# A fused attention and expert kernel: other PSUM banks and another engine for weights at the passage to the experts

## The chip, the cores and the metric

The kernel runs on one core of a Trainium2 chip as a single program. The metric is the device time of that program in microseconds (us). The core has five engines, each with a queue of its own that it works off in order: TensorE (PE, matmuls and transposes), VectorE (DVE), ScalarE (ACT), GpSimd (POOL) and SyncE (SP, which here only issues transfers). Matmul results go to PSUM, which is used here as eight banks of 512 columns; tiles of one tag in a pool share a fixed number of banks, so a new tile waits until the engine that reads the old one is done.

## The reference, cut to what matters

```
# 1. attention, B=4, 8 heads, S=576, head size 64; four heads see the last 32 positions,
#    four see the positions of their own residue modulo 32
x = softmax(mask(q @ k.T / 8)) @ v                     # -> (4, 576, 512)
# 2. mixing layer
theta = x @ w_theta;  zr = x * cos(theta);  zi = x * sin(theta)
y = w_tok_r @ zr + w_tok_i @ zi;  u = x + y
x = u + relu(u @ w_ch)                                 # (4, 576, 512)
# 3. four experts, each a causal attention with its own projections; two are chosen per position
logits = x @ w_gate;  chosen = the two largest;  w = softmax of the two
out = sum over chosen e of  w_e * (softmax(causal(q_e @ k_e.T / 8)) @ v_e @ wo_e)
```

## The kernel before

Most matmuls are carried out as three products of split operands: each operand is a high part, rounded to fp32r, and a low part, the rest. `mm3` issues high by high, high by low and low by high into one bank. Each high part is a copy on ACT or DVE, each low part a subtraction on DVE or POOL.

The program has two phases. In the first, the four batches b = 0 to 3 go through `theta` (angles), `rotate` (`xn` transposes, z), `tokens` (y, 27 matmuls into one bank of the tag "acc", which has two banks; each unit is evicted on DVE at L375 into X) and `channels` (g, evicted at L397). The attention of batch b+1 is interleaved in four pairs of heads (`attn_pair`): scores, exp on ACT (L227), transposes `tp` (L239), their copy `pt` on ACT (L243). The sine of `theta` and the exp lie in different tables of ACT, so that going from one to the other loads a table. In the second phase each batch goes through V products (`pv`, `project_v`), q and k products of two experts at a time (`pq_b_m_part_n`: m the pair of experts, part 0 q and part 1 k, n the half of the positions), and for each expert `attention` with scores s, masks, exp, transposes tp, values o; fills put products of later work between the score matmuls.

Between the phases lies the passage: while the last batch's `tokens` run, `load_split` brings in the weights wqk (four blocks of 512 columns) and wvg (four of 260: V and gate) through three stage buffers. SP issues a block's transfer when a buffer is free, ACT writes the high part (L106), and an engine writes the low part (L108), which frees the buffer. Then come the last `channels` units, the five V units of batch 0 (the fifth, `pv_4`, holds the ends of batches 0 and 1, and ACT copies the second as `v_end`), the choice of experts `gates(0)` on DVE, the q and k units of experts 0 and 1, and the weights wo. A q unit is evicted in four steps: ACT copies the first head's high part (L578), DVE writes its low part from the same bank (L579), and so again for the second head. A k unit goes the same way (L582, L583).

The order of the instructions on each engine is set by a planner that simulates the program; program text sets it only in part. `tc.issue_after(x)` adds the rule that the instructions in its block come after x in the queue of x's engine; it adds no wait between engines. Pools are opened and closed as stacks, and pool `ps2` of the second phase takes the banks that `ps1` of the first phase leaves, in the order in which its tags are first used: before, "acc" (two banks), "s" (three), "t" (two, for transposes), "o" (one), so that the V and q products take the banks in which the first phase's "acc" lay.

## Time and profile before

| | |
|---|---|
| runs | 548.86, 549.3 and 2792.86 us, median 549.3 |
| profiled execution | 548.84 us, span 547.1 us |
| mean granted TensorE clock | 0.982 |
| PE busy | 523.8 us (96% of the span) |
| DVE busy | 399.3 us (73%) |
| ACT busy | 316.8 us (58%) |
| POOL busy | 195.2 us (36%) |

The span runs from the first to the last instruction; 1.7 us of the execution lie outside it. Of the three runs two lie within 0.5 us of each other, and one is far off. A share of busy time is an average over all stages; of TensorE, 523.8 us of 547.1 us leave 23.3 us in which it did no work, and the views below show where some of these lie.

### The profile page before, as it was taken

How to read it: one execution, taken by the hardware profiler on the slowest of the kernel's cores; microseconds unless marked ns; L12 is line 12 of the kernel's file. 1: busy time of each engine (PE TensorE's matmuls, PEld its weight loads, DVE VectorE, ACT ScalarE, POOL GpSimd, SP SyncE). 2: the span in 40 equal slices, each digit the busy share in tenths (PEclk: the TensorE clock that was granted, in tenths of full speed). 3: DMA queues.
4: the chain of work that ended last, by engine and by line, in shares of the span. 5: the costliest groups of instructions: out<-in, count | busy, mean ns of one | idle time of the engine just before them, and what ended most of it. 6: DMA issues, size and time to landing. Idle time of an engine off the chain costs nothing.

```text
span 547.1 us, 12352 instructions
## 1 busy us (share of the span) xinstructions
PE 523.8 (96%) x4500; PEld 499.2 (91%) x4500; DVE 399.3 (73%) x1237; ACT 316.8 (58%) x874; POOL 195.2 (36%) x280
## 2 busy tenths in 40 slices
PE   6899889999999999999999999999999999999997
PEld 5788889999999999989999999879988998999987
DVE  6979997585847567756456443699998888888972
ACT  4878965336363263452145431587788757867873
POOL 5100023230643113542006453175456443625541
PEclk9859999999999999999999999999999999999999
DMA  9857255360202131000100021000001001100112
GB/s 269 280 186 261 61 183 160 112 205 1 87 6 88 34 134 34 23 23 15 46 0 2 3 58 40 1 1 2 1 22 54 14 2 44 45 2 10 36 46 88
DMA packets 20133, 36.62 MB, mean 67 GB/s; under 512 B 2648, under 2 KB 12040, under 8 KB 20072
## 3 DMA queue, kind: packets, MB, share of 16 engines
q1 hardware_dynamic: 20072, 35.83, 20.3%
q8 instruction: 36, 0.59, 0.5%
q14 instruction: 25, 0.20, 0.1%
HBM read 31.10 MB, written 4.72 MB: 65 GB/s over the span
## 4 chain that ended last, share of the span: by engine, by line
PE 72%; DVE 15%; ACT 6%; DMA 4%; issue 3%; POOL 0%; SPq 0%; DVEq 0%; ACTq 0%; POOLq 0%
PE y L290 6%; PE y L291 6%; PE y L292 6%; PE av L267 4%; PE g L290 3%; PE g L292 3%; PE g L291 3%; PE s L203 3%; PE tp L672 3%; PE tp L239 3%; PE th L290 3%; PE th L292 3%; PE th L291 2%; PE pq L290 2%; PE s L631 2%
## 5 line engine op out<-in xcount | busy, mean ns | idle before, releaser
L290 PE MATMUL y<-wtk_hi,zhi 128*128 128x288 f32 x288 | 86.0, 300 | 1.8 <-DVE X L375 1.2
L291 PE MATMUL y<-wtk_lo,zhi 128*128 128x288 f32 x288 | 85.5, 298 | 0.0
L292 PE MATMUL y<-wtk_hi,zlo 128*128 128x288 f32 x288 | 85.5, 298 | 0.0
L236 POOL TENSOR_TENSOR p<-p,sm 128x288 f32<-128x288 f32 (+2 forms) x36 | 22.6, 634 | 135.8 <-DVE sm L235 58.7
L667 POOL TENSOR_SCALAR p<-p,sm,gt 128x256 f32<-128x256 f32 (+3 forms) x63 | 44.9, 715 | 53.7 <-DVE sm L665 25.1
L290 PEld LDWEIGHTS y<-wtk_hi,zhi 128*128 128x128 f32 x288 | 54.0, 188 | 2.5 <-DVE X L375 1.6
L291 PEld LDWEIGHTS y<-wtk_lo,zhi 128*128 128x128 f32 x288 | 54.1, 188 | 0.1
L292 PEld LDWEIGHTS y<-wtk_hi,zlo 128*128 128x128 f32 x288 | 54.0, 188 | 0.0
L360 POOL TENSOR_TENSOR zlo<-cs,zhi 128x512 fp32r<-128x512 f32 (+1 forms) x30 | 36.0, 1213 | 49.0 <-DVE zhi L356 41.3
L290 PE MATMUL th<-wth_hi,x_hi 128*128 128x256 f32 (+1 forms) x160 | 47.6, 298 | 1.3 <-DVE cs L314 0.8
L291 PE MATMUL th<-wth_lo,x_hi 128*128 128x256 f32 (+1 forms) x160 | 45.6, 286 | 0.0
L292 PE MATMUL th<-wth_hi,x_lo 128*128 128x256 f32 (+1 forms) x160 | 45.2, 287 | 0.0
L286 POOL TENSOR_TENSOR x_lo<-X,x_hi 128x576 fp32r<-128x576 f32 x20 | 29.3, 1468 | 35.5 <-DVE x_hi L284 30.2
L243 ACT COPY pt<-tp 96x384 f32<-96x384 f32 (+2 forms) x44 | 21.1, 480 | 35.0 <-PE tp L239 34.5
L290 PE MATMUL pq<-x_hi,wqk_hi 128*128 128x288 f32 x128 | 39.6, 310 | 1.3 <-DVE q L579 1.1
L203 PE MATMUL s<-k,q 128*108 128x54 f32 (+2 forms) x320 | 40.3, 266 | 0.3 <-DMA v<-in_vs 0.3
L203 PEld LDWEIGHTS s<-k,q 128*108 128x108 f32 (+1 forms) x320 | 38.5, 188 | 0.8 <-POOL q L173 0.4
L290 PE MATMUL g<-u_hi,wch_hi 128*128 128x288 f32 x128 | 38.7, 302 | 0.0
L681 DVE TENSOR_TENSOR ptlo<-tp,pthi 128x128 fp32r<-128x128 f32 (+4 forms) x80 | 37.6, 479 | 1.1 <-ACT pthi L680 0.4
L291 PE MATMUL pq<-x_lo,wqk_hi 128*128 128x288 f32 x128 | 37.9, 296 | 0.0
L292 PE MATMUL pq<-x_hi,wqk_lo 128*128 128x288 f32 x128 | 37.8, 295 | 0.0
L291 PE MATMUL g<-u_lo,wch_hi 128*128 128x288 f32 x128 | 37.8, 295 | 0.0
(183 smaller groups left out, 1703.6 us busy)
## 6 DMA issues: line engine op xcount, KB each, us to landing
X<-in_wtk SPq DMA_DIRECT2D x8, 575.5 KB
q<-in_ql SPq DMA_DIRECT2D x7, 576.0 KB
q<-in_qs SPq DMA_DIRECT2D x6, 594.0 KB
v<-in_vl SPq DMA_DIRECT2D x24, 144.0 KB
out_t<-X SPq DMA_DIRECT2D x20, 128.0 KB
k<-in_kl SPq DMA_DIRECT2D x8, 304.0 KB
k<-in_ks SPq DMA_DIRECT2D x8, 288.0 KB
X<-in_wth SPq DMA_DIRECT2D x4, 511.5 KB
```

The lines of the kernel that those rows point to most:

```text
L203: nc.tensor.matmul(s[:rm, i * kw:i * kw + w], qt[:, j0 + i, :], kt[:, k0:k0 + w], start=False, stop=i == n - 1)
L236: (nc.vector if b == 0 else nc.gpsimd).tensor_tensor(tiles(p), tiles(p), each(sm), op=ALU.mult)
L239: turned = nc.tensor.transpose(tp[:kw, i * rm:(i + 1) * rm], p[:rm, i * kw:(i + 1) * kw], ident[:rm, :rm])
L243: copy(pt[:kw, :n * rm], tp[:kw, :n * rm])
L267: last = nc.tensor.matmul(av[64 * h:64 * h + 64, c0:c0 + wi], vg[:w, i, h, :], pt[:w, i, h, :wi], start=True, stop=True)
L286: halved[name] = eng.tensor_tensor(lo, x, f(hi), op=ALU.subtract).ins
L290: nc.tensor.matmul(ps, ahi, bhi, start=first, stop=False)
L291: nc.tensor.matmul(ps, ahi, blo, start=False, stop=False)
L292: return nc.tensor.matmul(ps, alo, bhi, start=False, stop=last)
L360: halved[b, h] = eng.tensor_tensor(lo, zf, f(hi), op=ALU.subtract).ins
L667: eng.tensor_scalar(p[:w, :kn], p[:w, :kn], sm[:w, t:t + 1], gt[:w, t, e:e + 1], op0=ALU.mult, op1=ALU.mult)
L681: nc.vector.tensor_tensor(dst(ptlo), src, f(dst(pthi)), op=ALU.subtract)
```

## The change

The change has five parts. Line numbers after it are one to three higher.

1. The k products of experts 0 and 1 of batch 0 go to the banks of tag "t" (the transposes') instead of "acc".
2. `gates(0)` comes behind the last low part of the first q unit pair, `lower[0, 0, 1]`, in DVE's queue.
3. `load_split` takes an engine; the low parts of wqk and wvg are written by VectorE, those of wo by GpSimd as before.
4. For b > 1 the exp of pair 3 comes behind the copy `pt` of pair 2, group 1, in ACT's queue.
5. A tile `first` of tag "t" is made ahead of all others in `ps2`, so that "t" takes the two banks that the first phase's "acc" had, and the V products take other banks.

```diff
--- before.py
+++ after.py
@@ -109,13 +109,13 @@
         else:
             nc.vector.scalar_tensor_tensor(lo, st, scale, f(hi), op0=ALU.mult, op1=ALU.subtract)
 
-    def load_split(pool, spool, src, kt, n, name):
+    def load_split(pool, spool, src, kt, n, name, eng):
         hi = pool.tile([128, kt, n], F32R, name=f"{name}_hi")
         lo = pool.tile([128, kt, n], F32R, name=f"{name}_lo")
         for c in range(kt):
             st = spool.tile([128, 512], F32, tag="stage", name=f"{name}_st{c}")
             nc.sync.dma_start(st[:, :n], src[:, c, :])
-            split_w(hi[:, c, :], lo[:, c, :], st[:, :n])
+            split_w(hi[:, c, :], lo[:, c, :], st[:, :n], 1.0, eng)
         return hi, lo
 
     def new_split(pool, kt, n, name):
@@ -148,7 +148,7 @@
 
         return b == 0 and pair != 2 or b == 1 and g == 0
 
-    ps_of, loaded, valued, halved, peaks, powers = {}, {}, {}, {}, {}, {}
+    ps_of, loaded, copied, valued, halved, peaks, powers = {}, {}, {}, {}, {}, {}, {}
 
     def load_pair(b, pair, ain, qbufs, kbufs):
         local = pair < 2
@@ -223,7 +223,8 @@
             else:
                 top = nc.vector.tensor_reduce(mx[:rm, :n], tiles(s), axis=AX.X, op=ALU.max).ins
                 nc.vector.tensor_tensor(tiles(p), tiles(s), each(mx), op=ALU.subtract)
-                with tc.issue_after(sins[b - 1, pair // 2]) if (b > 1 and pair % 2) else nullcontext():
+                with (tc.issue_after(sins[b - 1, pair // 2]) if (b > 1 and pair % 2) else nullcontext(),
+                      tc.issue_after(copied[b, 2, 1]) if (b > 1 and pair == 3) else nullcontext()):
                     power = nc.scalar.activation(p[:rm, :n * kw], p[:rm, :n * kw], AF.Exp, scale=SCALE).ins
                 if g == 0:
                     powers[b] = power
@@ -240,7 +241,7 @@
                                              ident[:rm, :rm])
             pt = apl.tile([128, 8 * RQ], F32, tag="pt", name=f"pt_{b}_{pair}_{g}")
             copy = nc.vector.tensor_copy if b == 0 and g == 1 else nc.scalar.copy
-            copy(pt[:kw, :n * rm], tp[:kw, :n * rm])
+            copied[b, pair, g] = copy(pt[:kw, :n * rm], tp[:kw, :n * rm]).ins
             done.append((j0, pt[:, :n * rm].rearrange("p (n h q) -> p n h q", n=n, h=2), wd, vg))
             if b == 0 or g == 2:
 
@@ -454,8 +455,8 @@
             wc = ctx.enter_context(tc.tile_pool(name="wc", bufs=1, side="right"))
             with tc.tile_pool(name="ws", bufs=3, side="right") as ws:
                 with tc.issue_after(turns[b, 1]):
-                    wqk_hi, wqk_lo = load_split(wc, ws, wqk, 4, 512, "wqk")
-                    wvg_hi, wvg_lo = load_split(wc, ws, wvg, 4, 260, "wvg")
+                    wqk_hi, wqk_lo = load_split(wc, ws, wqk, 4, 512, "wqk", nc.vector)
+                    wvg_hi, wvg_lo = load_split(wc, ws, wvg, 4, 260, "wvg", nc.vector)
             wm = ctx.enter_context(tc.tile_pool(name="wm", bufs=1, side="right"))
             identr, mask_cr = (wm.tile([128, 128], F32R, name=name) for name in ("identr", "mask_cr"))
             later = new_mask("later", [128, 640], wm)
@@ -482,9 +483,10 @@
     cw = ctx.enter_context(tc.tile_pool(name="cw", bufs=1))
     cp = ctx.enter_context(tc.tile_pool(name="cp", bufs=2))
     ps2 = ctx.enter_context(tc.tile_pool(name="ps2", bufs=2, space=PSUM))
-
-
-    xproj, vs, qks, moved = {}, {}, {}, []
+    ps2.tile([128, 512], F32, tag="t", name="first")
+
+
+    xproj, vs, qks, lower, moved = {}, {}, {}, {}, []
     klow = [[cw.tile([128, S], F32R, name=f"klow_{j}_{i}") for i in range(2)] for j in range(3)]
 
     def clear(j):
@@ -567,7 +569,7 @@
             ms = slice(256 * m + 128 * part, 256 * m + 128 * part + 128)
             sc = 1.0 / math.sqrt(HD) if part == 0 else 1.0
             sl = slice(HALF * n, HALF * (n + 1))
-            pq = ps2.tile([128, 512], F32, tag="acc", name=f"pq_{b}_{m}_{part}_{n}")
+            pq = ps2.tile([128, 512], F32, tag="t" if part and (b, m) == (0, 0) else "acc", name=f"pq_{b}_{m}_{part}_{n}")
             for c in range(4):
                 mm3(pq[:, :HALF], wqk_hi[:, c, ms], wqk_lo[:, c, ms], xproj[b][c][0][:, sl], xproj[b][c][1][:, sl],
                     c == 0, c == 3)
@@ -576,8 +578,8 @@
                 ps = pq[own, :HALF]
                 if part == 0:
                     nc.scalar.activation(q[i][own, sl], ps, AF.Copy, scale=sc)
-                    nc.vector.scalar_tensor_tensor(q[i][other, sl], ps, sc, f(q[i][own, sl]), op0=ALU.mult,
-                                                   op1=ALU.subtract)
+                    lower[b, m, n] = nc.vector.scalar_tensor_tensor(q[i][other, sl], ps, sc, f(q[i][own, sl]),
+                                                                    op0=ALU.mult, op1=ALU.subtract).ins
                 else:
                     moved.append(nc.scalar.copy(k[i][own, sl], ps).ins)
                     nc.vector.tensor_tensor(kl[i][own, sl], ps, f(k[i][own, sl]), op=ALU.subtract)
@@ -762,7 +764,8 @@
     clear(0)
     for u in units_qk(0, 0):
         u()
-    gates(0)
+    with tc.issue_after(lower[0, 0, 1]):
+        gates(0)
     for j in range(1, 3):
         clear(j)
 
@@ -771,7 +774,7 @@
             return cp.tile([128, 640], dtype, tag="p", bufs=4, name=name)
 
     with tc.issue_after(moved[-1]):
-        wo_hi, wo_lo = load_split(cw, PStage(), wo, 2, 512, "wo")
+        wo_hi, wo_lo = load_split(cw, PStage(), wo, 2, 512, "wo", nc.gpsimd)
     otp = None
     for b in range(B):
         done = [] if b == 0 else [partial(output, b - 1, otp, cut, m) for m in range(4) for cut in QCUT]
```

**ACT, attention of batch 3 during the tokens of batch 1** (`cs` and `zhi` are angles and z of the mixing layer, `p_3` the exp of pair 3, `pt_2` the copies of pair 2). Before:

```order
L327 ACTIVATE cs_1_4_3191<-cs_1_4_3191,halfpi 64x256
L328 ACTIVATE cs_1_4_3191<-cs_1_4_3191 64x256
L227 ACT_TABLE_LOAD
L227 ACTIVATE p_3_0_3495<-p_3_0_3495 108x216
L243 COPY pt_2_1_3259<-tp_2_1_3254 54x432
L227 ACTIVATE p_3_1_3518<-p_3_1_3518 108x216
L358 CAST zhi_1_1_3319<-cs_1_1_3140 128x512
```

After:

```order
L328 ACTIVATE cs_1_4_3191<-cs_1_4_3191,halfpi 64x256
L329 ACTIVATE cs_1_4_3191<-cs_1_4_3191 64x256
L244 COPY pt_2_1_3259<-tp_2_1_3254 54x432
L228 ACT_TABLE_LOAD
L228 ACTIVATE p_3_0_3495<-p_3_0_3495 108x216
L228 ACTIVATE p_3_1_3518<-p_3_1_3518 108x216
L359 CAST zhi_1_1_3319<-cs_1_1_3140 128x512
```

The copy `pt_2_1` has moved ahead of the table load and the first exp.

**DVE, tokens of the last batch, where the weights come in** (`y` are the banks of the token products, `u` their sum with x). Before:

```order
L375 TENSOR_TENSOR X_64<-y_1_1_4253,X_64 128x288
L352 TENSOR_TENSOR cs_1_4_4053<-xn_1_4_4099,cs_1_4_4053 64x256
L353 TENSOR_TENSOR cs_1_4_4053<-xn_1_4_4099,cs_1_4_4053 64x256
L356 CAST zhi_1_4_4102<-cs_1_4_4053 128x256
L385 TENSOR_TENSOR u_1_lo<-X_64,u_1_hi 128x288
L375 TENSOR_TENSOR X_64<-y_2_0_4294,X_64 128x288
L375 TENSOR_TENSOR X_64<-y_3_0_4323,X_64 128x288
L385 TENSOR_TENSOR u_2_lo<-X_64,u_2_hi 128x288
```

After:

```order
L353 TENSOR_TENSOR cs_1_4_4053<-xn_1_4_4099,cs_1_4_4053 64x256
L354 TENSOR_TENSOR cs_1_4_4053<-xn_1_4_4099,cs_1_4_4053 64x256
L108 TENSOR_TENSOR wqk_lo<-wqk_st_4119,wqk_hi 128x512
L357 CAST zhi_1_4_4102<-cs_1_4_4053 128x256
L108 TENSOR_TENSOR wqk_lo<-wqk_st_4123,wqk_hi 128x512
L108 TENSOR_TENSOR wqk_lo<-wqk_st_4127,wqk_hi 128x512
L386 TENSOR_TENSOR u_1_lo<-X_64,u_1_hi 128x288
L108 TENSOR_TENSOR wqk_lo<-wqk_st_4131,wqk_hi 128x512
L108 TENSOR_TENSOR wvg_lo<-wvg_st_4137,wvg_hi 128x260
L108 TENSOR_TENSOR wvg_lo<-wvg_st_4141,wvg_hi 128x260
L376 TENSOR_TENSOR X_64<-y_2_0_4294,X_64 128x288
L376 TENSOR_TENSOR X_64<-y_3_0_4323,X_64 128x288
```

Four low parts of wqk and two of wvg now stand ahead of the eviction of `y_2_0`; the other two of wvg stand a few rows further on, ahead of that of `y_2_1`. They have left POOL's queue.

**ACT, V and first q and k units** (`vc` high parts of V, `k` and `q` high parts of the units, `wo_hi` of the last weights). Before:

```order
L526 CAST vc_4571<-pv_2_4614 128x4x64
L526 CAST vc_4571<-pv_3_4630 128x4x64
L522 COPY v_end<-pv_4_4646 64x260
L526 CAST vc_4571<-pv_4_4646 64x4x64
L526 CAST vc_4994<-v_end 64x4x64
L578 ACTIVATE q_0_0_4665<-pq_0_0_0_4669 64x288
L578 ACTIVATE q_0_1_4666<-pq_0_0_0_4669 64x288
L578 ACTIVATE q_0_0_4665<-pq_0_0_1_4686 64x288
L549 ACTIVATE gt_4575<-lg_4572 128x20
L578 ACTIVATE q_0_1_4666<-pq_0_0_1_4686 64x288
```

After:

```order
L528 CAST vc_4572<-pv_2_4615 128x4x64
L528 CAST vc_4572<-pv_3_4631 128x4x64
L584 CAST k_0_0_4668<-pq_0_1_1_4723 64x288
L584 CAST k_0_1_4669<-pq_0_1_1_4723 64x288
L106 ACTIVATE wo_hi<-wo_st_4773 128x512
L106 ACTIVATE wo_hi<-wo_st_4777 128x512
L524 COPY v_end<-pv_4_4647 64x260
L528 CAST vc_4572<-pv_4_4647 64x4x64
L528 CAST vc_4995<-v_end 64x4x64
L580 ACTIVATE q_0_0_4666<-pq_0_0_0_4670 64x288
L580 ACTIVATE q_0_1_4667<-pq_0_0_0_4670 64x288
L580 ACTIVATE q_0_0_4666<-pq_0_0_1_4687 64x288
```

The k units have moved ahead of `pv_4`'s, and two of the copies of wo stand ahead of `v_end`. On DVE the gate operations of `gates(0)` now stand between the masks of the first expert and the low parts of the q units of experts 2 and 3 (`q_1_0`, `q_1_1`), which PE computes into the same two banks as the q units of experts 0 and 1; one stretch of that queue after the change reads:

```order
L581 SCALAR_TENSOR_TENSOR q_0_1_4667<-pq_0_0_1_4687,q_0_1_4667 64x288
L545 TENSOR_TENSOR cmp_4743<-lg_4573 128x5x3
L545 TENSOR_TENSOR cmp_4743<-lg_4573 128x5
L549 TENSOR_REDUCE mx_4757<-lg_4573 128x5
L637 ISA p_0_2_4852,nm_0_4786<-s_0_2_0_4853,later 128x384
L637 ISA nm_0_4786 128x1
L581 SCALAR_TENSOR_TENSOR q_1_0_4792<-pq_1_0_0_4796,q_1_0_4792 64x288
L547 TENSOR_TENSOR cnt_4742<-cnt_4742,cmp_4743 128x5x3
L547 TENSOR_TENSOR cnt_4742<-cnt_4742,cmp_4743 128x5
L637 ISA p_0_3_4894,nm_0_4786<-s_0_3_0_4895,later 128x512
L637 ISA nm_0_4786 128x1
L545 TENSOR_TENSOR cmp_4743<-lg_4573 128x5x2 x2
```

On PE the k units of experts 0 and 1 now come between the V units, the q units after the last V unit, and then scores and the q and k units of experts 2 and 3.

## Rows read from the trace of the kernel before

**Rows 1.** The page's first line of busy times by engine, whole span.

```profile
PE 523.8 (96%) x4500; PEld 499.2 (91%) x4500; DVE 399.3 (73%) x1237; ACT 316.8 (58%) x874; POOL 195.2 (36%) x280
```

**Rows 2.** What PE waited for: engine, tile, line, releaser: us in total, times, longest.

```profile
PE y L290 <- DVE X L375: 1.2, 2, 0.7
PE pq L290 <- DVE q L579: 1.1, 2, 0.7
```

**Rows 3.** Timeline of ACT and PE, batch 3's attention: start, us, instruction [idle before].

```profile
235.26 1.28 ACT L227 ACT_TABLE_LOAD   x1
...
236.84 0.50 ACT L243 COPY pt<-tp 54x432 f32<-54x432 f32 x1
...
237.48 0.44 PE L239 MATMUL tp<-ident,p 108*54 108x108 f32 x3 [1.08 <-ACT pt L243]
```

**Rows 4.** Timeline where the weights come in: ACT, POOL, SP's queue, DVE, PE.

```profile
316.45 0.63 ACT L106 ACTIVATE wqk_hi<-wqk_st 128x512 fp32r<-128x512 f32 x1 [3.02 <-DMA wqk_st<-in_wqk]
...
318.92 0.42 ACT L106 ACTIVATE wvg_hi<-wvg_st 128x260 fp32r<-128x260 f32 x1 [0.71 <-DMA wvg_st<-in_wvg]
...
312.14 2.54 POOL L108 TENSOR_TENSOR wqk_lo<-wqk_st,wqk_hi 128x512 fp32r<-128x512 f32 x2 [0.75 <-ACT wqk_hi L106]
...
313.46 0.33 SPq L117 DMA_DIRECT2D wqk_st<-in_wqk  x1
...
316.86 1.95 SPq L117 DMA_DIRECT2D wvg_st<-in_wvg  x2
...
313.46 1.54 DVE L385 TENSOR_TENSOR u_lo<-X,u_hi 128x288 fp32r<-128x288 f32 x1 [1.89 <-ACT u_hi L384]
316.20 0.82 DVE L375 TENSOR_TENSOR X<-y,X 128x288 f32<-128x288 f32 x2 [1.20 <-PE y L292]
...
326.18 0.46 DVE L385 TENSOR_TENSOR u_lo<-X,u_hi 128x288 fp32r<-128x288 f32 x1 [1.07 <-ACT u_hi L384]
...
316.71 0.40 PE L290 MATMUL y<-wtk_hi,zhi 128*128 128x288 f32 x1 [0.42 <-DVE X L375]
```

**Rows 5.** DVE's groups by shape: count | busy us, mean ns | idle before.

```profile
L579 DVE SCALAR_TENSOR_TENSOR q<-pq,q 64x288 fp32r<-64x288 f32 x32 | 14.6, 455 | 1.0
...
L635 DVE CUSTOM_DVE_ANT_0 p<-s,later 128x512 f32<-128x512 f32 x8 | 5.5, 682 | 0.6 <-POOL olo L706 0.5
...
L360 DVE TENSOR_TENSOR zlo<-cs,zhi 128x512 fp32r<-128x512 f32 x8 | 5.4, 680 | 0.0
...
L512 DVE TENSOR_TENSOR xeolo<-X,xeohi 128x256 fp32r<-128x256 f32 x4 | 1.6, 419 | 0.1
...
L543 DVE TENSOR_TENSOR cmp<-lg 128x15 f32<-128x15 f32 x8 | 1.3, 164 | 0.0
```

**Rows 6.** Timeline of the passage: PE, then ACT.

```profile
337.45 0.39 PE L290 MATMUL pv<-wvg_hi,x_hi 128*128 128x260 f32 x1 [0.55 <-DVE X L397]
...
346.37 0.37 PE L290 MATMUL pq<-x_hi,wqk_hi 128*128 128x288 f32 x1
...
347.92 0.29 PE L292 MATMUL pq<-x_hi,wqk_lo 128*128 128x288 f32 x1
348.90 0.37 PE L290 MATMUL pq<-x_hi,wqk_hi 128*128 128x288 f32 x1 [0.69 <-DVE q L579]
...
344.95 0.37 ACT L522 COPY v_end<-pv 64x260 f32<-64x260 f32 x1 [1.07 <-PE pv L292]
...
347.60 0.41 ACT L578 ACTIVATE q<-pq 64x288 fp32r<-64x288 f32 x1 [0.67 <-DVE q L579]
...
354.80 1.15 ACT L106 ACTIVATE wo_hi<-wo_st 128x512 fp32r<-128x512 f32 x2
```

**Rows 7.** Windows: length, busy us (instructions) PE, PEld, DVE, ACT, POOL, granted clock, DMA, GB/s.

```profile
36.10:39.40 3.30, 3.26 (x15) 3.26 (x16) 3.17 (x5) 2.67 (x5) 0.00 (x0) 0.50 0.78 252
39.40:42.60 3.20, 3.20 (x28) 3.20 (x28) 3.11 (x7) 1.92 (x4) 0.00 (x0) 0.98 1.04 313
...
360.00:380.00 20.00, 19.29 (x140) 16.95 (x139) 18.51 (x75) 16.74 (x48) 12.18 (x18) 1.00 0.00 1
```

## Prediction

> **What bounds the kernel now.** I read the busy line first, then the view of what PE waits for, then the timeline at each place that the change touches. TensorE is busy for 523.8 of 547.1 us, and no other engine is above 73% [rows 1]. So PE's own work sets the time, and an edit counts only as far as it takes away, moves or adds idle time of PE; an engine that merely works more costs nothing until PE waits for it. The change leaves PE's matmuls as they are. The waits that it can reach are short: one of 1.08 us at a copy [rows 3], 1.2 in two places for the eviction of y and 1.1 in two places for the low parts of q [rows 2], and 0.55 ahead of the first V product [rows 6]. All of them together are under 4 us, 0.7% of the time; what the change could win lies inside that, and what it could lose lies in the waits that it makes. Close to PE stands VectorE in one stretch: from 360 to 380 us it is busy for 18.51 of 20 us [rows 7], so that lost time there is hardly regained.
>
> **The copy ahead of the exp: -1.1.** PE waits 1.08 us for the copy pt of pair 2, which ACT starts at 236.84, behind a table load of 1.28 us and one exp [rows 3]. In the changed order the copy stands ahead of both, and the tile that it reads has been written well before. The wait goes; the exp is later by one copy, 0.3 to 0.5 us, and PE has the token products of batch 1 to do meanwhile. Bounds: -1.2 to 0. The rule also holds for batch 2, where the trace has no wait of this kind; zero there.
>
> **Low parts of wqk and wvg on VectorE: +1.8.** The work itself is cheap: a subtraction of 128x512 took VectorE 0.68 us and one of 128x256 0.42 [rows 5], against 1.27 on POOL [rows 4]. What counts is what stands behind them. In the new order the eviction of y_2_0, which frees the bank that PE's next unit y_2_1 is to take, is behind all four low parts of wqk and two of wvg. These follow transfers:
> - ACT's first high part is done by 312.14, where POOL starts on it now [rows 4]. VectorE's low part ends at 312.1 + 0.68 = 312.8 and frees the first stage buffer; POOL freed it at 313.4, and SP issued the fourth transfer at 313.46 [rows 4]. It is now issued at about 312.85.
> - From that issue to ACT's copy 2.99 us passed (313.46 to 316.45) [rows 4]: now 315.84. The copy takes 0.63, the low part 0.68: 317.15.
> - The two low parts of wvg, 0.42 each, follow at once, since their transfers need about 2.06 us from issue to copy (316.86 to 318.92) [rows 4] and their buffers are free by 314.6: 317.97.
> - Then the eviction, 0.41 to 0.45: 318.4, and PE starts y_2_1 at about 318.5.
>
> Now PE starts it at 316.71, with 0.42 us of waiting [rows 4]. So 318.5 - 316.7 = +1.8. PE has nothing between the end of y_3_0 and y_2_1 that could fill the gap. The last two parts of wvg stand ahead of the eviction of y_2_1, but that unit takes 27 matmuls, each step about 0.14 us at most ((347.92 - 346.37)/11 for products of the same 288 columns [rows 6]), 3.6 us, and they are done by then: nothing. POOL gets rid of eight instructions and waits for no one: nothing. Bounds: -0.55, if the weights are there early (then even the present wait goes), to +2.15.
>
> The upper bound takes in a row: a low part u_lo on VectorE took 1.54 us while POOL was in its subtraction of wqk, and 0.46 with POOL idle [rows 4]. The moved low parts may meet POOL's last zlo in the same way; I put that at a third of the 1.08 us between the two rows, 0.35, since it can only reach the first of them. The Trainium skill's page "SBUF — State Buffer", section "Who interferes with whom", says that a VectorE instruction with two SBUF inputs and a GpSimd instruction that reads SBUF hold a shared port in turn, each for its whole length. By it this term would be +2.15. I take +1.8, because by the time that the fourth low part comes POOL has nothing left to do.
>
> **V in other banks: -0.55.** The first V product waits 0.55 us for the eviction of the last g [rows 6]; in other banks it does not. Bounds -0.6 to 0.
>
> **k units in the transposes' banks, gates behind q: +1.8.** Gone are the waits of the k units for the low parts of q, 1.1 in two places [rows 2, 6] (0.98 us from 347.92 to 348.90 is the longer one, 0.84 more than a step; with the other, both cost 1.2). New are four:
> - *v_end behind wo_hi.* ACT's two copies of wo, 1.15 us [rows 6], now stand ahead of v_end and of the copy of V from pv_4's bank. The second q unit takes that bank. Counted from the end of pv_4: ACT reaches v_end some 1.3 us after, its copies and the two steps of VectorE last another 1.3, and PE has one unit of 1.6 (12 steps) to do: a wait of 1.1.
> - *First q unit of experts 2 and 3 (0.2), third unit (0.65), fourth (1.1).* The units for q_1 take the two banks of q_0. A bank comes free after a chain of four steps, ACT, VectorE, ACT, VectorE, of 0.41 and 0.46 us each: the second ACT step waits 0.67 for VectorE already now [rows 6]. That is some 2.1 us against 1.6 of PE's for the unit between and 0.5 for two scores: 0.2. For the next banks VectorE has the masks p_0_2 and p_0_3 (up to 0.68 [rows 5]) and some 20 small operations of the gates (0.16 each or less, since they overlap [rows 5]) between the low parts. Going through the order row by row I get the third bank free 0.65 us after PE wants it, and the fourth 1.1 after.
>
> Together 3.05 - 1.2 = +1.8. Bounds: -1.2, if the planner's order lets VectorE run ahead, to +2.5.
>
> **Sum**: -1.1 + 1.8 - 0.55 + 1.8 = +1.95, against the profiled execution's 548.84, which is 0.5 below the median 549.3: **550.8 us**, 0.35% more than now.
>
> **Rivals.**
> - *Half of it, no change (548.9).* The passage costs nothing, because VectorE regains there what the gates cost later: they have to be done somewhere, and now they stand between q's low parts too. For it: PE also has gaps from 363 to 371 that may shrink. Against: VectorE is almost full there [rows 7]. -1.1 + 1.8 - 0.55 + 0.
> - *Not slower: 545.5.* The waits that I derive from the order are not there, since the weights land early and the gates find gaps: -1.1 - 0.55 - 0.55 - 1.1 = -3.3. For it: every old wait named above is real and has its own edit. Against: the transfer's 2.99 us is a row, and the order puts the eviction behind it. It decides on one point, whether the fourth transfer is in by 315.0.
> - *Clearly slower: 552.4 and up.* The gap ahead of y_2_1, some 2.3 us, is twice as long as the 1.08 us of rows 3, and the clock might fall. Near the start the granted clock was at 0.50 (1.2 GHz) and rose to 2.4 GHz only after 3.3 us in which PE was busy throughout: 15 matmuls at 0.22 us, where in the next 3.2 us 28 took 0.114 each [rows 7], a price of 15 x 0.106 = 1.6 us. 550.8 + 1.6 = 552.4. It decides if 2.3 us without matmuls is enough to lower the clock, which no row shows. The page "TensorE: Matmul & The Clock Gate" of the Trainium skill, Part 1, says that the clock follows how busy the engine has lately been; by it the price falls due at that gap and at no other.
>
> **How the numbers follow.** Forecast 0.45, no change 0.22, not slower 0.18, clearly slower 0.13, 0.02 for something far off: the changed order of PE and VectorE up to 455 us that I did not follow. The range of 8 in 10 goes from 546.0, inside the third case, to 553.0, which takes in the fourth; the forecast's own range is 549.7 to 551.8. Two per cent are 11 us, about what a measurement can tell from no change; no case reaches that, so same gets 0.96, faster 0.015 and slower 0.025.
>
> **What would show it.** In the changed profile: no wait of tp for pt near 236 us; the eviction of y_2_0 behind wvg's low parts at about 318, and a PE wait of some 2 us ahead of y_2_1; no wait of the first pv for X; a wait of the second q unit for pv_4's bank of about 1 us, with wo_hi on ACT ahead of v_end; waits of the third and fourth q_1 and k_1 units for low parts of q_1. I am wrong if the wait at y_2_1 is below 1 us, if the clock falls there, or if VectorE's gates cost the q units nothing.

## The result, and the profile after

| | before | after |
|---|---|---|
| median | 549.08 us (548.66, 548.86, 549.3, 2792.86) | 555.35 us (553.63, 554.7, 555.99, 556.14) |
| profiled execution | 548.84 us, span 547.1 | 554.70 us, span 552.6 |
| mean granted clock | 0.982 | 0.978 |

The ratio is 1.0116, 95% interval [1.0091, 1.014]: 6.3 us slower. I predicted 550.8 with 546.0 to 553.0 as the range; the time lies above it.

The first line of busy times of the changed kernel answers to [rows 1]:

```profile
PE 525.3 (95%) x4500; PEld 502.3 (91%) x4500; DVE 402.0 (73%) x1245; ACT 316.5 (57%) x874; POOL 187.4 (34%) x272
```

TensorE runs as many instructions as before in 1.5 us more busy time, while the span grew by 5.5 us: most of the loss is idle time, and a small part is instructions that took longer. PE's waits in the changed kernel (columns as in [rows 2]) name the places:

```profile
PE y L291 <- DVE X L376: 2.9, 2, 2.1
PE pq L291 <- DVE q L581: 2.1, 3, 1.0
...
PE po L291 <- ACT X L736: 1.8, 1, 1.8
...
PE pq L291 <- DVE lg L530: 1.0, 1, 1.0
```

The waits of y and pq I had named. The wait of `po`, a product of the output, is at 425 us, and the prediction has no term for it.

**Where the time went.** I compared the starts of the same PE matmuls in the two profiles. The later one starts are (after minus before, in the execution's own time):

| place | lag, us | by this step | what lies there |
|---|---|---|---|
| ~125 us | -0.64 | -0.64 | nothing of the change; this differs from profile to profile |
| behind the copies of batches 2 and 3 | -2.11 | -1.47 | -0.21 and -1.26 |
| start of y_2_1 | -0.40 | +1.71 | low parts of the weights ahead of the eviction |
| g at 324 us | +1.12 | +1.5 | matmuls at a lowered clock |
| ~410 us | +3.5 | +2.4 | passage, choice of experts, first experts |
| 436 us | +6.28 | +2.8 | the `po` wait and matmuls at a lowered clock |
| ~485 us to the end | +5.58 | -0.7 | regained |

The +2.4 up to 410 us is not the passage alone. PE's waits of 0.1 us and more ahead of q and k units grew from 0.84 us in two places to 2.25 in four. Those behind them, from 364 to 402 us, grew from 1.11 to 2.93: the longest are 0.74 for a mask on VectorE at 384, 0.64 for a low part of x on POOL at 369 and 0.59 for a low part on VectorE at 368. Not all of this waiting shows in the lag.

**The copy.** On ACT in batch 3 the copy now stands ahead of the table load, and PE has no wait there as in [rows 3]:

```profile
234.31 0.50 ACT L244 COPY pt<-tp 54x432 f32<-54x432 f32 x1
234.83 1.28 ACT L228 ACT_TABLE_LOAD   x1
```

**The weights.** The same stretch as [rows 4]: SP's issue of the fourth transfer, ACT's high part of it, VectorE's low parts, the eviction, PE.

```profile
310.71 0.33 SPq L117 DMA_DIRECT2D wqk_st<-in_wqk  x1
...
313.81 0.63 ACT L106 ACTIVATE wqk_hi<-wqk_st 128x512 fp32r<-128x512 f32 x1 [2.49 <-DMA wqk_st<-in_wqk]
...
314.47 0.69 DVE L108 TENSOR_TENSOR wqk_lo<-wqk_st,wqk_hi 128x512 fp32r<-128x512 f32 x1 [1.48 <-ACT wqk_hi L106]
315.08 0.81 DVE L108 TENSOR_TENSOR wvg_lo<-wvg_st,wvg_hi 128x260 fp32r<-128x260 f32 x2
315.80 0.81 DVE L376 TENSOR_TENSOR X<-y,X 128x288 f32<-128x288 f32 x2
...
316.31 0.54 PE L291 MATMUL y<-wtk_hi,zhi 128*128 128x288 f32 x1 [2.13 <-DVE X L376]
```

3.10 us pass from the issue to ACT (before 2.99), then the low part, two low parts of wvg, and only then the eviction. Ahead of the fourth low part, two others took 1.83 us together, for one of them stood beside POOL's last subtraction of z:

```profile
310.80 1.83 DVE L108 TENSOR_TENSOR wqk_lo<-wqk_st,wqk_hi 128x512 fp32r<-128x512 f32 x2
...
310.96 1.11 POOL L361 TENSOR_TENSOR zlo<-cs,zhi 128x256 fp32r<-128x256 f32 x1 [1.68 <-DVE zhi L357]
```

One took 0.68 us and the other 1.22. It cost nothing here, since VectorE then waited for the fourth transfer. PE waits 2.13 us ahead of y_2_1 where it waited 0.42. The windows behind that wait (columns as in [rows 7]) show a second cost:

```profile
314.00:316.30 2.30, 0.18 (x2) 0.00 (x0) 1.83 (x5) 1.18 (x4) 0.00 (x0) 1.00 0.15 44
316.30:319.60 3.30, 3.29 (x14) 3.29 (x15) 2.00 (x5) 1.92 (x5) 0.79 (x2) 0.52 0.26 75
319.60:323.00 3.40, 3.40 (x26) 3.40 (x26) 0.77 (x2) 0.73 (x2) 0.13 (x1) 0.97 0.02 5
...
425.10:428.00 2.90, 2.90 (x12) 2.58 (x13) 2.35 (x8) 1.49 (x5) 2.50 (x4) 0.59 0.29 100
```

After 2.3 us almost without matmuls the granted clock is 0.52 (near 1.2 GHz) and PE gets through 14 matmuls in the time of some 25; then it is back at 2.4 GHz. The same happens at 425 us, at 0.59.

**The passage.** ACT and PE, where [rows 6] showed them:

```profile
338.57 0.39 PE L291 MATMUL pv<-wvg_hi,x_hi 128*128 128x260 f32 x1 [0.55 <-DVE X L398]
...
349.13 1.15 ACT L106 ACTIVATE wo_hi<-wo_st 128x512 fp32r<-128x512 f32 x2
350.19 0.35 ACT L524 COPY v_end<-pv 64x260 f32<-64x260 f32 x1
...
351.85 0.37 PE L291 MATMUL pq<-x_hi,wqk_hi 128*128 128x288 f32 x1 [1.04 <-DVE lg L530]
...
359.59 0.37 PE L291 MATMUL pq<-x_hi,wqk_hi 128*128 128x288 f32 x1 [0.37 <-DVE q L581]
...
362.14 0.37 PE L291 MATMUL pq<-x_hi,wqk_hi 128*128 128x288 f32 x1 [0.74 <-DVE q L581]
```

The first V product waits exactly as before. The second q unit waits 1.04 us, for ACT has copied wo ahead of `v_end`; two later q units wait 0.37 and 0.74.

**At 425 us.** ACT's casts of batch 2's x, and PE's products of the output on both sides of them. In the kernel before, where this lies at 416 us:

```profile
415.87 0.66 ACT L282 CAST x_hi<-X 128x576 fp32r<-128x576 f32 x1
...
418.94 0.42 ACT L734 COPY X<-po 128x320 f32<-128x320 f32 x1
...
416.75 0.31 PE L290 MATMUL po<-ohi,wo_hi 128*128 128x320 f32 x1
...
419.41 0.39 PE L290 MATMUL po<-ohi,wo_hi 128*128 128x256 f32 x1 [0.41 <-ACT X L734]
```

After:

```profile
422.00 1.82 ACT L283 CAST x_hi<-X 128x576 fp32r<-128x576 f32 x3
423.73 0.39 ACT L584 CAST k<-pq 64x288 fp32r<-64x288 f32 x1
424.02 0.67 ACT L283 CAST x_hi<-X 128x576 fp32r<-128x576 f32 x1
424.59 0.42 ACT L736 COPY X<-po 128x320 f32<-128x320 f32 x1
...
421.07 0.30 PE L291 MATMUL po<-ohi,wo_hi 128*128 128x320 f32 x1
...
425.06 0.39 PE L291 MATMUL po<-ohi,wo_hi 128*128 128x256 f32 x1 [1.85 <-ACT X L736]
```

In both kernels four casts of x and a copy of k stand ahead of the copy that frees a bank for the next `po`. Before, the casts began 0.88 us ahead of the first matmul of the `po` that is to be copied, spread between exps, and the copy came 2.19 us behind that matmul. After, two of ACT's copies that came behind the casts (of o and of a tile's transposes) stand ahead of them; the casts begin 0.93 us behind that matmul, with no exp between, and the copy comes 3.52 us behind it. PE waits 1.85 us instead of 0.41.

### The profile page after: what moved, and what is told of

It reads as the page before. It is cut to its first block, busy times and chain, and to the rows that moved or that the text cites. A ratio compares the mean times of both kernels' runs of the same rounds, so it can differ in the third digit from the quotient of the medians.

```text
span 552.6 us, 12341 instructions
## 1 busy us (share of the span) xinstructions
PE 525.3 (95%) x4500; PEld 502.3 (91%) x4500; DVE 402.0 (73%) x1245; ACT 316.5 (57%) x874; POOL 187.4 (34%) x272
## 4 chain that ended last, share of the span: by engine, by line
PE 74%; DVE 13%; ACT 4%; DMA 4%; issue 2%; POOL 1%; SPq 0%; DVEq 0%; ACTq 0%; POOLq 0%
PE y L291 6%; PE y L292 6%; PE y L293 6%; PE av L268 4%; PE g L291 3%; PE s L203 3%; PE tp L674 3%; PE g L293 3%; PE g L292 3%; PE th L291 3%; PE tp L240 3%; PE th L293 3%; PE th L292 3%; PE pq L291 3%; PE s L633 2%
```

## The experiments

All kernels below compute the full result. Medians stand against runs of the kernel before on the same chip. The edits of the change are called **engine** (part 3, for wqk and wvg), **k banks** (1), **gates** (2), **copy** (4) and **first** (5).

**e1, engine alone**, in the kernel before:

```diff
-            split_w(hi[:, c, :], lo[:, c, :], st[:, :n])
+            split_w(hi[:, c, :], lo[:, c, :], st[:, :n], 1.0, eng)   # nc.vector for wqk, wvg
```

> The kernel before with one part of the change, the low parts of wqk and wvg on VectorE. Theory: the wait ahead of y_2_1 becomes 2.1 us (from 0.42, so +1.7), and behind it the granted clock falls to about 0.5 for some 3.3 us (+1.5): 3.2 us more than before, about 552.3. Rival 1, the clock costs nothing that the wait doesn't: +1.7, 550.8. Rival 2, the loss lies with the experts and not here: within 0.5 of before.

Measured: 552.19 against 548.49, 1.007 [1.0051, 1.0089]. PE's row and the window behind it:

```profile
320.23 0.40 PE L290 MATMUL y<-wtk_hi,zhi 128*128 128x288 f32 x1 [2.24 <-DVE X L375]
...
320.20:323.50 3.30, 3.27 (x24) 3.27 (x25) 2.03 (x5) 1.94 (x5) 0.87 (x2) 1.00 0.25 75
```

The wait is there, and behind it the clock stays at 1.00. The engine costs 3.7 us by the medians and 1.8 at y in the profile. The profile is 3.7 us longer than that of the kernel before all the same, for its clock fell near 80 us, behind waits of 1.07 and 0.74 us that the kernel before has there too (1.01 and 0.74). Its lag grows by 1.5 us at that place, which no part of the change touches:

```profile
79.50:82.90 3.40, 3.40 (x16) 3.40 (x16) 2.75 (x9) 2.49 (x7) 1.31 (x2) 0.50 0.35 126
```

**e2, engine with a filler**: e1 and 14 matmuls into an idle bank, issued behind y_3_0, so that PE does not pause.

```diff
+                if (b, m, n) == (B - 1, 3, 0):
+                    with tc.issue_after(ended.ins):
+                        stream(ps1.tile([128, 512], F32, tag="av", bufs=2, name="busy"), 14, ...)
```

> As the run with the engine alone, and PE carries out 14 more matmuls of 288 columns into an unused bank (1.86 us in sum) behind y_3_0, while y_2_1 waits; the other engines' order is the same. Theory: y_2_1 starts no earlier, but the clock stays at 1.00, so that the 1.5 us of the slow stretch are won back: 550.8, 1.5 less than with the engine alone. Rival, the slow stretch is not due to PE's idleness (a fall that comes anyway): 552.3, no difference. Rival 2, the filler delays y_2_1: more than the engine alone.

Measured: 551.05 against 548.49, 1.0051 [1.0037, 1.0065], 1.1 less than e1, though the intervals overlap. PE:

```profile
315.39 2.01 PE L94 MATMUL busy<-wtk_hi,zhi 128*128 128x288 f32 x14
...
317.76 0.40 PE L290 MATMUL y<-wtk_hi,zhi 128*128 128x288 f32 x1 [0.36 <-DVE X L378]
```

y_2_1 starts 1.8 us later than before all the same: that part is the order of VectorE, and no clock. Behind y the profiles of e1 and e2 run alike, since the clock did not fall there in either.

**e3, the change without the engine**: `nc.gpsimd` again for wqk and wvg.

> The changed kernel with the low parts of wqk and wvg back on GpSimd. Theory: the loss at y_2_1 and the slow stretch behind it go (-3.2), the waits in the passage and the wait of po near 425 stay: about 552.1, with the clock lower near 425 alone. Rival, VectorE's load is what slows the experts, so that less of it helps there too: below 551.

Measured: 552.23, 1.0065 [1.0043, 1.0086]; 3.1 less than the change. The y wait is 0.42 again. At 425 us the wait is 1.85 as in the change, and the clock falls:

```profile
420.00:440.00 20.00, 19.06 (x137) 18.19 (x138) 16.63 (x69) 14.29 (x43) 9.92 (x16) 0.91 0.07 25
```

So more than half of the loss, 3.7 of 6.3 us, is there without the engine.

**e4, copy alone.**

> The kernel before with one part of the change, the copy of pair 2 ahead of the exp of pair 3. Theory: the wait of 1.08 us near 237 goes and nothing takes its place: -1.2, about 547.9. Rival, the gain is taken back later by the exp that is late or by the changed order: 549.1.

Measured: 546.95 against 548.49, 0.9973 [0.9962, 0.9983]: -1.5. In the profile -0.21 in batch 2 and -1.22 in batch 3, kept to the end.

**e5, k banks alone** (the tag "t" for the first k products, without first and gates).

> The kernel before with one part of the change, the first k products in the transposes' banks. Theory: this part alone brings all of the loss behind the weights, because with the k units ahead ACT's copies of wo stand ahead of v_end, and the order of the experts changes up to 455 us, with the same wait of po for ACT near 425: a wait of 1.0 us for pv_4's bank, 1.85 at po and in some runs a slow stretch behind it; 3 to 4.5 us more than before, 551.5 to 553. Rival, the gates bring it and this part alone gains the 1.1 us of the k units' old waits: 547.4.

Measured: 556.58 against 548.43, 1.0134 [1.0117, 1.0152]: +8.1, more than either theory gave. PE waits 1.04 for pv_4's bank, 0.40, 0.28 and 0.16 in the passage, 1.33 for a mask at 393 us, and 1.84 at `po`:

```profile
424.52 0.58 PE L290 MATMUL po<-ohi,wo_hi 128*128 128x256 f32 x1 [1.84 <-ACT X L734]
...
420.00:440.00 20.00, 17.77 (x116) 16.64 (x115) 15.31 (x52) 13.91 (x39) 10.53 (x15) 0.83 0.09 31
```

In this profile the low clock at `po` lasted twice as long as in e3 behind the same wait (0.83 over these 20 us, against 0.91). The tag of two products reorders ACT 70 us further on.

**e6, gates alone.**

> The kernel before with one part of the change, gates(0) behind the last low part of the first q units. Theory of the k banks: small, within 0.7 of before (548.5), since the experts' order stays as before from 400 us on. Rival, the gates between the masks and low parts of q_1 cost 1.8 us: 550.3.

Measured: 548.72 against 548.43, 1.0011 [0.9998, 1.0024]: no cost by itself.

**e7, the change with the copy of `po` ahead of the casts.**

```diff
+            with tc.issue_after(brought[0, 2, 256]) ...:      # batch 2's x_hi on ACT
                 nc.scalar.copy(hi, x)
```

> The changed kernel, and ACT's high parts of batch 2's x come behind the copy of the output bank po (output of batch 0, third block, second half). Theory: the wait of po of 1.85 us near 425 goes, and with it the slow stretch: 2 to 3 us less than the changed kernel, 552.3 to 553.3. Rival, VectorE and ACT are full there and the wait turns up at the next bank: within 0.7 of the changed kernel's 555.35.

Measured: 553.59, 1.0097 [1.0079, 1.0114], 1.8 less than the change. Waits of 0.39 and 0.28 take the place of the 1.85. At y PE still waits 2.22, and the clock does not fall there in this profile, which is 1.4 us of its lead over the change's; another 1.4 come at `po`. The time lies 0.3 above the expected range.

**e8, copy and k banks, wo late**: the kernel before with the two edits, and ACT's copies of wo behind the last high part of q.

```diff
-    with tc.issue_after(moved[-1]):
+    with tc.issue_after(moved[-1]), tc.issue_after(raised[-1]):   # raised: ACT's q high parts
```

> The kernel before with the copy ahead of the exp, the first k products in the transposes' banks, and wo's copies on ACT held back until the last high part of the first q units as well; no other part. Theory: without wo ahead of v_end the k banks win back the old waits of 1.1 us, and the copy its 1.4: 546.0. Rival, the loss in the passage comes from VectorE's low parts and masks, whatever ACT does: 547 or above, no better than the copy alone (546.95).

Measured: 546.25 against 548.43, 0.9962 [0.995, 0.9974]. Of the passage's waits 0.24 and 0.30 are left, and PE is 0.73 faster through it than before. ACT's order at `po` is that of the kernel before again, with a wait of 0.39. The k banks are no loss in themselves; the copies of wo that they let ACT bring forward are, there and 70 us on.

**e9, k banks with a filler**: e5 and 13 matmuls into unused columns of a transposes' bank ahead of `po`.

> As the run with the k banks alone (556.58), and PE carries out 13 more matmuls of 288 columns (1.7 us in sum) in the unused columns of the bank of tp_2_0, where it waits 1.84 us for po's bank near 425. The planner orders some instructions between 425 and 455 us anew. Theory: po starts no earlier, but the clock stays at 1.00 from 420 to 440 (0.83 without), which gives back 1.5 to 2.5 us: 554 to 555. Rival, the clock falls all the same, or its fall costs nothing: 556 to 557.

Measured: 554.36 against 548.55, 1.009 [1.0062, 1.0118], 2.2 less than e5. PE, and the window:

```profile
424.87 1.95 PE L94 MATMUL tp<-wqk_hi 128*128 128x288 f32 x13
...
426.96 0.39 PE L290 MATMUL po<-ohi,wo_hi 128*128 128x256 f32 x1
...
420.00:440.00 20.00, 19.47 (x152) 18.31 (x151) 18.06 (x66) 16.61 (x49) 11.94 (x17) 1.00 0.09 31
```

With work in the gap the clock stays at 1.00 there, and the time falls by somewhat more than the 1.5 us of one fall; e5's lasted twice as long. The planner's new order from 425 to 455 us may have a part in it. In this profile the clock fell elsewhere (near 79 us, and 0.91 from 360 to 380).

**e10, the change with wo late** (the edit of e8).

> The changed kernel, and wo's copies on ACT held back until the last high part of the first q units as well. Theory: the wait for pv_4's bank (1.04 us) goes, the experts' order is then such that the wait of po near 425 and its slow stretch don't come about, and what is left is the weights' loss of 3.3 less the copy's 1.4: 550 to 551. Rival, the passage is slow because of VectorE's gates and low parts: 553 or above.

Measured: 554.88, 1.011 [1.008, 1.0139]: missed by 4 us. The wait for `v_end`'s bank is gone, and a new one of 2.14 us came, for a mask that stands behind the gates in VectorE's queue; the clock falls behind it. VectorE, POOL, PE and the window:

```profile
354.29 0.26 DVE L545 TENSOR_TENSOR cmp<-lg 128x15 f32<-128x15 f32 x2
354.54 1.35 DVE L547 TENSOR_TENSOR cnt<-cnt,cmp 128x15 f32<-128x15 f32 x2
355.82 1.32 DVE L545 TENSOR_TENSOR cmp<-lg 128x10 f32<-128x10 f32 x2
...
354.52 2.60 POOL L108 TENSOR_TENSOR wo_lo<-wo_st,wo_hi 128x512 fp32r<-128x512 f32 x2 [5.70 <-issue]
...
358.64 0.34 PE L633 MATMUL s<-k,q 128*64 128x288 f32 x1 [2.14 <-DVE nm L637]
...
358.60:362.00 3.40, 3.00 (x13) 2.75 (x14) 3.21 (x17) 2.44 (x7) 0.23 (x2) 0.66 0.02 5
```

Pairs of tiny operations of the gates take 1.35 and 1.32 us, for the whole of one of POOL's two subtractions of wo each, and 0.26 just before POOL starts. With the wo copies late, these subtractions fall on the gates; in the change POOL is done with them at 352.4 us, and the gates' compares start at 356.4.

**e11, e8 and the first three low parts of wqk on VectorE.**

```diff
+            split_w(hi[:, c, :], lo[:, c, :], st[:, :n], 1.0, nc.vector if c < early else nc.gpsimd)   # early = 3
```

> The run with copy, k banks and late wo (546.25), and the first three low parts of wqk on VectorE, the fourth and all of wvg on GpSimd as before, so that no eviction stands behind a transfer that is still under way. Theory: the eviction of y_2_0 no longer waits for a low part that GpSimd holds up, and PE's wait of 0.42 us ahead of y_2_1 goes: 545.7. Rival, three low parts on VectorE are late enough to keep the eviction waiting: 546.25 or more.

Measured: 546.68 against 548.55, 0.9958 [0.9943, 0.9972]. The wait ahead of y_2_1 is gone (-0.39 in the profile), but the median is not the 545.7 that was expected, and by the medians this and e8 can't be told apart. Both beat both kernels.

**e12, the change with wo late and only these three low parts on VectorE.**

> The changed kernel with both mendings: wo late, and only the first three low parts of wqk on VectorE, the rest on GpSimd. Theory: all five parts then gain or cost nothing: 545.5 to 546.5, as the best without the gates. Rival, the gates behind q cost something of their own: 547 or above.

Measured: 551.98, 1.0056 [1.0038, 1.0075]: missed. Again 2.12 us for the mask behind the gates, with POOL in wo's low parts, and the clock at 0.58 behind it.

**e13, the change with both fillers.**

> The changed kernel with both fillers: 14 more matmuls of PE while y_2_1 waits, and 13 more while the output bank po waits near 425. No wait ends sooner; the planner orders some instructions between 425 and 455 anew. Theory: a lowered clock behind these two waits costs 2.5 to 3.5 of the changed kernel's 6.3 us: 551.8 to 552.9. Rival, the lowered clock is rare or costs little, and the rest of the loss lies elsewhere: 554.5 or above.

Measured: 554.32 against 548.84, 1.0102 [1.008, 1.0123]: only 1.0 less than the change, missed. Its profile (552.74) is 1.96 less than the change's, in the expected range, with the clock at 1.00 from 40 us to 547. Matmul by matmul it is 1.5 us ahead of the change's behind y and another 1.5 behind `po`, and gives back 1.0 by 460 us. Of the other runs one is as short (552.72). Two of 554.9 and 555.2 have a mean clock of 0.979, against 0.982 and 0.983 for the two short ones, which points to a fall somewhere. The last two (554.3) have 0.982, and why they are longer isn't known.

**e14, the change without the k banks** (all k products in "acc").

> The changed kernel with the first k products back in the banks of the V and q products; the gates stay behind q. Theory: all of the loss behind 340 us goes, since ACT has v_end ahead of wo again and po's wait near 425 does not arise: copy -1.5, weights +3.7, gates +0.3, in sum 551.0. Rival, the gates make a wait in the passage with the other parts, too: 553 or above.

Measured: 550.28 against 548.84, 1.0021 [1.0007, 1.0036], 5.1 less than the change. The `po` wait is 0.36; at y PE waits 2.26 with the clock at 1.00 there.

**e15, e12 with wo's low parts on VectorE too.**

```diff
-        wo_hi, wo_lo = load_split(cw, PStage(), wo, 2, 512, "wo", nc.gpsimd)
+        wo_hi, wo_lo = load_split(cw, PStage(), wo, 2, 512, "wo", nc.vector)
```

> The change mended (551.98), and wo's low parts on VectorE instead of GpSimd, so that GpSimd has nothing to do while the gates run. Theory, the pairs of compares and counts took 1.35 and 1.32 us because GpSimd's subtractions of wo shut them out: they take 0.25 now, the wait of 2.14 us ahead of the scores s falls to about 1.0 although VectorE has 1.4 us more of its own work there, and the clock stays: 549 to 550. Rival, VectorE's queue is what delays the mask: the 1.4 us come on top, the wait is 2.1 or more, 552 or above.

Measured: 550.43 against 548.56, 1.0035 [1.002, 1.005], 1.55 less than e12 and 0.4 above the expected range. VectorE and PE:

```profile
352.53 0.25 DVE L547 TENSOR_TENSOR cnt<-cnt,cmp 128x15 f32<-128x15 f32 x2
...
354.38 0.24 DVE L545 TENSOR_TENSOR cmp<-lg 128x10 f32<-128x10 f32 x2
...
354.51 0.34 PE L633 MATMUL s<-k,q 128*64 128x288 f32 x1 [0.61 <-DVE nm L637]
```

The pairs are back at 0.25 us, although VectorE now has two subtractions more, and PE's wait is 0.61 instead of 2.12.

**e16, the change without first.**

```diff
-    ps2.tile([128, 512], F32, tag="t", name="first")
```

> The change without the tile `first`: the V and q products take the first phase's acc banks again, and nothing else differs; the order on PE, DVE and ACT is the same. Theory, the tile moves nothing: as the changed kernel, 555.4 within 1, and the wait ahead of the first V product is 0.55 as with it. Rival, the banks matter at that place or later: a V wait other than 0.55 and, if the gates and po waits hang on them, 553.5 or less.

Measured: 554.14 against 548.97, 1.01 [1.0074, 1.0125]; 0.3 below the expected band; the intervals of this and of the change overlap. V waits 0.55 in other banks or in the same. PE's order and waits are those of the change, which makes it a test of the clock as well. PE at y, at V and at `po`, and the windows behind the first and the last:

```profile
316.50 0.40 PE L291 MATMUL y<-wtk_hi,zhi 128*128 128x288 f32 x1 [2.14 <-DVE X L376]
...
338.76 0.39 PE L291 MATMUL pv<-wvg_hi,x_hi 128*128 128x260 f32 x1 [0.55 <-DVE X L398]
...
425.26 0.39 PE L291 MATMUL po<-ohi,wo_hi 128*128 128x256 f32 x1 [1.84 <-ACT X L735]
...
316.50:319.80 3.30, 3.30 (x18) 3.30 (x19) 1.99 (x5) 1.92 (x5) 0.73 (x2) 0.70 0.26 79
...
425.30:428.20 2.90, 2.90 (x20) 2.73 (x21) 2.84 (x9) 1.70 (x6) 2.52 (x4) 1.00 0.29 102
```

`po` starts 0.20 later than in the change's profile and the span ends 1.3 earlier: after the same wait the clock fell in one profile (0.59) and not in the other (1.00), and 1.5 us lie between them.

**e17, first alone**, in the kernel before.

> The kernel before with the tile `first` alone. Theory, the tile moves nothing: 548.7 within 0.6, and the V wait is still 0.55. Rival, the prediction's own step: the wait goes, 548.2, 0.5 less. A wait that stays here says that what it waits for is not the old bank of the first phase's acc.

Measured: 548.77 against 548.97, 1.0 [0.9981, 1.002], and V waits 0.55.

## Why the prediction was wrong

- **The copy: right.** -1.1 was said; -1.5 by the runs of e4, and -1.22 to -1.26 at that place in the profiles. Batch 2, put at zero, gave 0.21.
- **The low parts on VectorE: the wait right, its price too small.** +1.8 was the forecast of y_2_1's start and +1.7 to +1.8 came, by the chain given. One moved low part did meet POOL and took 1.22 us instead of 0.68, but it was the third, not the first, and VectorE idled 1.48 us behind it for the fourth transfer: the 0.35 of the upper bound were not paid. The price of the clock, 1.6 in the rival "clearly slower", was 1.5 in the profile of the change. That rival was given 0.13; in six profiles with this wait and no filler (2.1 to 2.3 us: the change, e1, e7, e10, e14, e16) the clock fell in two. By the runs the engine costs 3.1 (e3 against the change) to 3.7 (e1), which is the two terms together. The sum left this term out, and the clock fell not "at that gap and at no other", but at `po` as well, and in e1 near 80 us. What one fall costs is shown by profiles of the same order with and without it: 1.5 us at y (the change and e13) and 1.5 at `po` (the change and e16). How much of the engine's 3.1 to 3.7 it makes up in the mean of the runs isn't shown: e2's 1.1 us only point to it, and some 0.8 of e2's excess over the kernel before has no place.
- **V in other banks, -0.55: failed.** The tile `first` had nothing to do with the wait: it is 0.55 with `first` and without, in both kernels (e16, e17). That `first` moves the banks follows from the order in which the pool takes them; no row shows a bank. In the profiles SP's transfers of wo and a memset of POOL start right behind the last g product, and PE's V behind the last eviction of g, whichever banks V takes. That fits a release of the first phase's pools as a whole; a run that tells this from another cause wasn't made.
- **The passage, +1.8: the waits right, the net less, and more behind it.** The wait behind wo_hi was 1.04 (said 1.1), those of the q units 0.37 and 0.74 (said 0.65 and 1.1, and 0.2). Less the old waits, PE waits 1.4 us more there (said 1.8). To 410 us the lag grew by 2.4, and the rest of it lies in the waits behind the passage, for which the prediction has no term; e8 and e14 do not have them. The prediction took its 1.8 for the price of k banks and gates together. By e8 the k banks cost nothing when wo is late and the gates stay where they were, and by e6 the gates alone cost nothing. Together with the k banks the gates do cost some: the waits of the first, third and fourth of those q and k units are 0.40, 0.28 and 0.16 in e5 without them, and 0.10, 0.37 and 0.74 in the change.
- **The step that failed by most** is the one put down as "the changed order of PE and VectorE up to 455 us that I did not follow", at a chance of 0.02. It was ACT's order in the main: one copy that came later against PE, behind four casts, cost 1.85 us of waiting (before 0.41) and the clock behind it, 2.8 us in all at 436, of which 0.7 came back. The waits between 364 and 402 us are the smaller part. e5 shows that the k banks alone bring it, e14 that it goes with them, e8 that wo late undoes it, and e7 that to put that one copy ahead of the casts takes 1.8 us off. Why the planner puts the casts later there isn't settled.

The runs' sum: copy -1.5, engine +3.1, k banks +5.1 (e14), gates +0.3, first about 0: +7.0, for 6.3 measured. The edits are not independent: wo late is worth 8.8 us on the k banks alone (e5 to e8, without the copy's 1.5) and 0.5 on the whole change (e10), where it brings POOL's subtractions onto the gates.

How often the clock falls in the runs without a profile can be read in part from the mean granted clock of each run. A fall like those shown lowers the mean by 0.003 (an estimate: half of 3.3 us over 550). Of 101 runs of the kernel before, 11 have 0.979 or 0.980 and took 550.2 to 550.8 us; the median of the others is 548.4. At 0.980 or below lie three of the change's four runs, four of e5's five, all four of e16, two of e13's six, five of e14's twelve and none of e2's six, e8's eight and e15's twelve. These counts are no more than a lower bound, since the mean takes in the slow stretch at the start, which was 17.1 us in some profiles and 13.7 in others. What stays open is the exact number of falls, why e13's median gives back so little, and what in a run decides about a fall.

One sum of the prediction is off by 0.1: the rival "no change" adds up to 549.0, not 548.9.

## What to carry to other kernels

When an edit puts an instruction that waits for a transfer on an engine, look for the eviction that stands behind it in that queue. When an edit frees a bank earlier, follow each engine's order to the end of the program: what is brought forward may stand ahead of an eviction, there or 70 us on. A pause of TensorE of some 2 us can cost most of its length again, so price it as a chance and not as nothing.

## What the runs showed of the hardware

**The clock after a pause.** After waits of 1.84 to 1.85 us at `po` without a filler the granted clock fell in three profiles of four (the change, e3 and e5, not e16), after those of 2.1 to 2.3 at y in two of six, and after those of 2.12 and 2.14 for the mask in two of two. With matmuls in the gap it stayed at 1.00 there (e2, e9, e13). It fell near 80 us as well, behind two waits of 1.1 to 1.5 and 0.7 us (e1, e8, e9), which are 1.0 and 0.7 in the kernel before, without a fall. A fall costs about 1.5 us (e1 near 80, the change against e13 at y and against e16 at `po`). The Trainium skill's page "TensorE: Matmul & The Clock Gate", Part 1, says that the clock is set by how busy the engine has lately been; these traces agree, and show besides that the same wait in the same order can go either way.

**VectorE and GpSimd.** Pairs of operations of 128x5 to 128x15 took 0.25 us without GpSimd and 1.3 us beside its subtraction of 128x512 (e10, e15); one of the two was held each time. In the change a low part of wqk took 1.22 us instead of 0.68 beside GpSimd's subtraction of 128x256. The Trainium skill's page "SBUF — State Buffer", section "Who interferes with whom", states that such instructions lock each other out for a whole instruction; these rows agree, and in e10 this turned operations of less than 0.2 us into a wait of 2.14 us on PE.
